# One output product by seven quarter products for tokens 512 to 1023, a rewritten first block, and two small edits in the gated products

## The chip, the cores and the metric

The kernel runs on one core of a Trainium2 chip. A core has TensorE (PE in the profile, with PEld for its weight loads) for matrix products, VectorE (DVE), ScalarE (ACT) and GpSimd (POOL) for element-wise work, and SyncE (SP), which issues the transfers here. The metric is the device time of one execution in microseconds. Three runs of the kernel before took 305.69, 305.70 and 306.51 us, median 305.7.

## The reference

Retention over 8 batches of 8 heads, 576 positions and 64 dimensions gives x, 4608 tokens of 512 values. A gated layer follows. In short:

```python
scores = q @ k.transpose(0, 1, 3, 2) / np.sqrt(64)
gamma = 1.0 - 2.0 ** (-5.0 - np.arange(8))
x = (scores * where(rel >= 0, gamma ** rel, 0)) @ v      # rel = i - j
gate = 1.0 / (1.0 + np.exp(-(x @ w_gate)))               # w_gate 512 x 1536
out = (gate * (x @ w_val)) @ w_out                       # w_val 512 x 1536, w_out 1536 x 512
```

All inputs and the output are float32 in memory; the products run on bfloat16 operands with float32 accumulation.

## The kernel before, in words

The sequence is cut into steps of 128 positions of one batch. Each step casts k, q and v (`casts_to`, lines 419 to 445), turns k and q with a DMA transposition on SP's queue or on TensorE (`turn_step`, L629), and takes part in an attention slot (`slot_of_two`, L739): "rows" are the scores within a step, "new" is what a step adds to the running state, "val" the values from the scores and from the state. These are matmuls of 64×64 tiles. After a slot, ScalarE casts the values off PSUM into x (`xT`, L780 and L786), and VectorE adds the states up (`add_state`, L827).

The gated layer goes over blocks of tokens. The first 512 tokens are done plainly: for each of 12 slices of 128 hidden columns, a gate product and a value product with 512 tokens each (`h_both`), a sigmoid on ScalarE into a tile `gv`, a multiplication on VectorE into the same tile, and then four output products of 12 matmuls with 512 columns (`op_first`). Tokens 512 to 767 and 768 to 1023 are two blocks of 256: `h_units` makes gates and values in pairs of slices, `op_units` makes two output products of 12 matmuls of 512 columns for each block and stores them. From token 1024 on the blocks have 512 tokens, and every product of four quarters is done as seven products of quarters on sums of operands, after Strassen and Winograd: `quarter_units` for gate ("g") and value ("w"), `quarters` (L1103) for the output. For these the operands have sums of their own: of x (`xsum`, L967), of the weights (`w_sums`, `wo_sums`, L364 and L323) and of gv (`gsum`, L941), each given to VectorE or to POOL.

In `quarters`, product 1 gathers in the bank qa. ScalarE copies it (L1177) into a second bank, qe, on which products 2, 5 and 3 go on adding, while 6, 7 and 4 go on in qa. VectorE adds the two banks to kept parts of products and leaves the output tile `ob`. The products come out in halves of six matmuls, and between halves other work can be put.

The order on each engine is the order in which the program writes the instructions. A run through the blocks takes one piece after the other out of `ffn_units`, and tables say what is put behind which piece: PAIRS_AT the attention slots of the first two small blocks, SUMS_AT the casts ("c"), turns ("t") and weight sums behind a piece, FIRST, ORDER and FINAL the sequence of gate and value quarters of a block of 512 ("g05" is the fifth product of the first unit of four slices; "0-1v" behind a colon is a sum of gv on VectorE), LATER and its like the sums of gv between output products. SP's queue holds loads, DMA transpositions and stores in one order.

In `quarter`, ScalarE's copy of the first product and a sigmoid that an earlier product left in `waiting` stand next to each other: `settle()` empties that list, and but for one place runs ahead of the copy.

## Time and profile before

| What | us |
|---|---|
| median of three runs | 305.7 |
| the profiled execution | 305.75 |
| its span, first to last instruction | 304.0 |
| granted TensorE clock, mean | 0.999 |
| TensorE busy | 296.8 |
| weight loads busy (beside it) | 250.0 |
| VectorE, ScalarE, POOL busy | 227.0, 204.9, 225.4 |

In the profile a group row reads: start, duration, engine, line, operation, output<-input, shape, count; what stands in brackets is how long the engine stood idle just before and what ended that. A group of pipelined matmuls lasts longer than the distance to the next group's start, since the last one's result comes some time after its last column; distances between starts say what a group keeps TensorE for. The first 21 us load and prepare; tokens 512 to 1023 are done between about 55 and 89 us, and the blocks of 512 tokens, some 30 us each, from 89 us to the end.

### The profile page before, as it was taken

The numbers are of one execution on the slowest core, as the hardware profiler recorded it, in microseconds if no ns is written. First come the engines' busy times: TensorE is split into PE (matmuls) and PEld (weight loads), VectorE is DVE, ScalarE is ACT, GpSimd is POOL, SyncE is SP. The second block draws the span as 40 slices with busy tenths as digits, with TensorE's granted clock in tenths as the row PEclk, the third lists the DMA queues.
The fourth block names the chain that finished last, engine by engine and source line by source line (L and its number), as shares of the span: only waits on it lengthen the run. The fifth ranks groups of instructions, "written<-read, shape, count | busy, mean of one in ns | idle before, by whom it ended". The sixth has DMA issues, their size and how long they took to land.

```text
span 304.0 us, 10670 instructions
## 1 busy us (share of the span) xinstructions
PE 296.8 (98%) x4429; PEld 250.0 (82%) x4437; DVE 227.0 (75%) x424; ACT 204.9 (67%) x414; POOL 225.4 (74%) x252
## 2 busy tenths in 40 slices
PE   8999999999999999999999999999999999999994
PEld 7677655978868888888888888888888888888884
DVE  5957776786886898588948983896489848945793
ACT  6755464335369657985798589857985698559830
POOL 5676544845679888999998999699969946960780
PEclk9999999999999999999999999999999999999999
DMA  7999999969999979998659966976694155004013
GB/s 212 303 360 394 316 351 220 209 149 204 200 198 203 262 133 222 223 205 237 99 125 213 261 144 141 228 188 141 122 201 132 38 119 195 4 2 138 2 37 104
DMA packets 145440, 54.99 MB, mean 181 GB/s; under 512 B 124400, under 2 KB 137712, under 8 KB 145392
## 3 DMA queue, kind: packets, MB, share of 16 engines
q1 hardware_dynamic: 144304, 53.59, 72.8%
q10 hardware_dynamic: 1088, 0.72, 0.8%
q8 instruction: 34, 0.56, 0.8%
q14 instruction: 14, 0.11, 0.1%
HBM read 37.75 MB, written 9.44 MB: 155 GB/s over the span
## 4 chain that ended last, share of the span: by engine, by line
PE 82%; POOL 7%; SPq 3%; DVE 3%; DMA 2%; issue 2%; ACT 1%; POOLq 0%
PE gatea L1013 10%; PE wa L1013 10%; PE qa L1136 9%; PE qe L1136 8%; PE gatee L1013 5%; PE we L1013 5%; PE h_v L884 4%; PE h_g L884 3%; PE op L1485 3%; PE hg L1335 3%; PE hv L1335 3%; SPq L186 3%; PE gateg L1013 3%; PE op L1267 3%; PE wg L1013 2%; DMA wg<-in_moe_w_gate_dram 2%
## 5 line engine op out<-in xcount | busy, mean ns | idle before, releaser
L1013 PEld LDWEIGHTS <-wg_sb 128*128 128x128 bf16 x336 | 32.9, 98 | 4.0
L1037 POOL TENSOR_TENSOR gv<-gv,wu 128x512 bf16<-128x512 bf16 x20 | 24.1, 1206 | 15.3 <-DVE wu L1050 15.3
L1136 PEld LDWEIGHTS <-gsum 128*128 128x128 bf16 x312 | 29.9, 98 | 3.7
L428 POOL TENSOR_TENSOR qk<-q,qtab 128x512 bf16<-128x512 f32 x28 | 30.2, 1079 | 2.7 <-DMA q<-in_q_dram 2.6
L1013 PEld LDWEIGHTS <-wv_sb 128*128 128x128 bf16 x296 | 28.9, 98 | 3.4
L1050 DVE TENSOR_TENSOR gu<-gatee,gu 128x512 f32<-128x512 f32 x21 | 14.5, 691 | 22.7 <-ACT gateg L1041 10.8
L1013 PEld LDWEIGHTS <-wgt_sb 128*128 128x128 bf16 x252 | 24.6, 98 | 3.7 <-issue 0.5
L941 POOL TENSOR_TENSOR gsum<-gsum,gv 128x256 bf16<-128x256 bf16 (+1 forms) x20 | 18.0, 911 | 12.8 <-DVE gsum L941 11.0
L1013 PE MATMUL gatea<-xsum,wg_sb 128*128 128x256 bf16 x168 | 25.0, 273 | 0.0
L1136 PEld LDWEIGHTS <-gv 128*128 128x128 bf16 x228 | 21.4, 98 | 3.5 <-DVE gv L1037 0.9
L428 POOL TENSOR_TENSOR qk<-k,ktab 128x512 bf16<-128x512 f32 x11 | 11.6, 1059 | 14.9 <-DMA k<-in_k_dram 12.6
L941 POOL TENSOR_TENSOR gsum<-gv,gsum 128x256 bf16<-128x256 bf16 (+1 forms) x24 | 21.9, 924 | 0.2
L702 DVE TENSOR_TENSOR pt<-row,tri 128x512 bf16<-128x512 f32 x30 | 19.2, 682 | 3.0 <-PE row L685 2.7
L1053 DVE TENSOR_TENSOR gs<-gatea,gs 128x512 f32<-128x512 f32 x21 | 14.5, 689 | 8.9 <-PE gatea L1013 8.8
L941 DVE TENSOR_TENSOR gsum<-gv 128x512 bf16<-128x512 bf16 (+1 forms) x34 | 19.9, 610 | 1.5 <-POOL gv L1037 1.5
L441 POOL TENSOR_TENSOR v<-v,ktab 128x512 bf16<-128x512 f32 x19 | 20.5, 1080 | 0.0
L657 ACT CAST sb<-s 128x512 bf16<-128x512 f32 (+1 forms) x26 | 14.4, 568 | 8.9 <-DVE s L827 8.7
L1013 PE MATMUL wa<-xsum,wv_sb 128*128 128x256 bf16 x136 | 20.4, 273 | 0.0
L786 ACT CAST xT<-val 128x512 bf16<-128x512 f32 x26 | 14.7, 592 | 6.8 <-PE val L732 6.8
L1013 PEld LDWEIGHTS <-wvt 128*128 128x128 bf16 x168 | 16.4, 98 | 2.1 <-issue 0.2
L1037 POOL TENSOR_TENSOR gv<-gv,ws 128x512 bf16<-128x512 bf16 x14 | 16.3, 1170 | 1.6 <-DVE ws L1053 1.4
L941 POOL TENSOR_TENSOR gsum<-gv 128x256 bf16<-128x256 bf16 (+1 forms) x20 | 17.5, 875 | 0.0
(202 smaller groups left out, 880.0 us busy)
## 6 DMA issues: line engine op xcount, KB each, us to landing
k<-in_k_dram SPq DMA_DIRECT2D x26, 256.0 KB, 3.9
q<-in_q_dram SPq DMA_DIRECT2D x26, 256.0 KB, 4.3
v<-in_v_dram SPq DMA_DIRECT2D x26, 256.0 KB, 4.9
out_dram<-ob SPq DMA_DIRECT2D x24, 256.0 KB, 2.9
wg<-in_moe_w_gate_dram SPq DMA_DIRECT2D x12, 256.0 KB, 5.5
wv<-in_moe_w_val_dram SPq DMA_DIRECT2D x12, 256.0 KB, 5.1
wo<-in_moe_w_out_dram SPq DMA_DIRECT2D x12, 256.0 KB, 5.3
v32p<-in_v_dram SPq DMA_DIRECT2D x6, 256.0 KB, 4.5
```

The lines of the kernel that those rows point to most:

```text
L428: eng.tensor_tensor(out=to, in0=by_halves(loaded[s][1 - i]), in1=tab, op=ALU.mult)
L441: nc.gpsimd.tensor_tensor(out=natural["v", s], in0=loaded[s][2], in1=tab, op=ALU.mult)
L702: nc.vector.tensor_tensor(out=t[:, y, 0:n].rearrange("p i m t -> p (i m) t"), in0=rows_tile[ss[0]][y][:, 0:n].rearrange("p i m t -> p (i m ...
L786: nc.scalar.copy(out=to, in_=src)
L884: nc.tensor.matmul(ps[:, i], lhsT=w_sb[:, kc, (fc + i) * P:(fc + i + 1) * P], rhs=xT(kc, slice(t0, t0 + n)), start=(kc == 0), stop=(kc == ...
L941: eng.tensor_tensor(out=to, in0=a, in1=b, op=op)
L1013: nc.tensor.matmul(ps[:, f], lhsT=w[:, kc, f * P:(f + 1) * P], rhs=x[:, kc], start=(first and f == 0 and kc == 0), stop=(f == 1 and kc == ...
L1037: eng.tensor_tensor(out=to, in0=to, in1=src, op=ALU.mult)
L1050: nc.vector.tensor_tensor(out=me["u2"], in0=e, in1=me["u2"], op=ALU.add)
L1053: nc.vector.tensor_tensor(out=me["s5"], in0=a, in1=me["s5"], op=ALU.add)
L1136: nc.tensor.matmul(ps[:, b], lhsT=left(fp)[:, b * P:(b + 1) * P], rhs=right(fp), start=(first and fp == 0 and b == 0), stop=(fp == NFC // ...
L1335: nc.tensor.matmul(ps[:, cols], lhsT=(wg_sb if what == "g" else wv_sb)[:, kc, fc * P:(fc + 1) * P], rhs=xT(kc, cols), start=(kc == 0), sto ...
```

## The change

Tokens 512 to 1023 still have their gates and values made in two blocks of 256, but into one common gv tile of 512 tokens. After the second block's gates and values one `quarters` call makes the output of all 512 tokens with seven products; `op_units` is gone. The sums of gv for it follow a new table, JOINT_AT. The slots of these tokens go by a table GROUPS: rows and new of steps 0 and 1, then the values of 0 and 1 by themselves, then rows and new of 2 and 3, and two slots of values and rows. The first block's program is one table of items, EARLY_AT, executed by `early`: D and d are a gate and a value product, C and o weight casts, "+" and "*" weight sums, p an output product, S, Z, I, J, X parts of the attention, s a store. Loads, casts and sums of steps 1 to 11 move (AHEAD, V_LATER, SUMS_AT), loads get fewer shared tiles from step 5 on, and sf's copies go to ScalarE.

Two edits concern the blocks from 1024 on: for products 1 and 5 of the first value unit (w0), ScalarE's copy now stands ahead of the waiting sigmoid (`behind_copy`), and the multiplication of product 4 of the third value unit (w24) is done in two halves.

```diff
-            t = landing([P, H, D], f"{nm}32_{s}", s >= 8)
+            t = landing([P, H, D], f"{nm}32_{s}", s >= 5)
...
-                (nc.vector.tensor_copy if hh == y else nc.sync.dma_start)(
+                (nc.scalar.copy if hh == y else nc.sync.dma_start)(
...
-    AHEAD = (2, 2, 1, 1, 0, 1, 1, 0, 1, 2, 1, 1)
+    AHEAD = (0, 3, 0, 0, 1, 1, 2, 0, 4, 3, 1, 0)
...
         for fc in fcs[::2]:
-            gv_tile(gvs, t0, fc)
-            both = made[t0, fc // 4][:, fc % 4:fc % 4 + 2, 0:n]
+            gv_tile(gvs, FIRST_PAIR, fc)
+            both = made[FIRST_PAIR, fc // 4][:, fc % 4:fc % 4 + 2, t0 - FIRST_PAIR:t0 - FIRST_PAIR + n]
...
-            if i != 1 or t0 != BLOCKS[2][0]:
+            behind_copy = i in (1, 5) and (t0 == BLOCKS[2][0] and i == 1 or (kind, u) == ("w", 0))
+            if not behind_copy:
                 settle()
...
-            def leaves(r, h, src, eng=nc.vector):
-                to = made[t0, u][:, 2 * r:2 * r + 2, h * 256:(h + 1) * 256]
-                if kind == "g":
-                    nc.scalar.activation(out=to, in_=src, func=AF.Sigmoid)
-                else:
-                    eng.tensor_tensor(out=to, in0=to, in1=src, op=ALU.mult)
+            def leaves(r, h, src, eng=nc.vector, parts=1):
+                for n in range(parts):
+                    part = slice(2 * n // parts, 2 * (n + 1) // parts)
+                    to = made[t0, u][:, 2 * r:2 * r + 2, h * 256:(h + 1) * 256][:, part]
+                    if kind == "g":
+                        nc.scalar.activation(out=to, in_=src[:, part], func=AF.Sigmoid)
+                    else:
+                        eng.tensor_tensor(out=to, in0=to, in1=src[:, part], op=ALU.mult)
...
-                leaves(1, 0, a)
+                leaves(1, 0, a, parts=2 if (kind, u) == ("w", 2) else 1)
+            if behind_copy:
+                settle()
...
-    FIRST = ("g01 g05 g11 w05 g06 g15 g03 w01 g02 g16 g12 g07 w06 g13 g21 g17 w03 w11 w07 g14 g04 w02 w04 "
...
+    FIRST = ("g01 g11 g05 w05 g06 g15 g03 w01 g16 g02 g12 g07 w06 g13 g17 g21 w03 w11 w07 g14 g04 w02 w04 w12 "
...
+    JOINT_AT = ("3:0-1v 4:0-2v 6:0-3v 8:0-4v 9:1-1v 12:2b1v 12:1-2v 13:2a1v 14:2a2p 14:2b2p 14:2-3p 15:1-4v "
+                "19:1-3p 20:2-4p").split()
...
-    def op_units(gvs, t0, n):
-        for nb in range(n // P):
...
-            gvs = {}
-            yield from h_units(gvs, range(NFC), t0, n)
-            yield from op_units(gvs, t0, n)
+            gvs = begun.setdefault(FIRST_PAIR, {})
+            sums = {}
+            for i, cols in enumerate(h_units(gvs, range(NFC), t0, n)):
+                behind(FIRST_PAIR, sums, JOINT.get((t0, i), ()))
+                yield cols
+            if t0 != FIRST_PAIR:
+                for i, cols in enumerate(quarters(gvs, sums, FIRST_PAIR, 2)):
+                    behind(FIRST_PAIR, sums, JOINT.get((t0, NFC + i), ()))
+                    yield cols
...
-    CUTS = 50
+    CUTS = 30
...
+    EARLY_AT = ("D2 D3 +g00v d3 Cv41v Cv43v d2 Cv40p D4 Cv42p D7 D5 +g01v +g03p D6 Cg81a Cg80p Cg82v Cg83v d4 "
...
+                "p5.0 p5.1 p5.2 p6.0 p6.1 p6.2 p7.0 p7.1 p7.2 p8.0 p8.2 p9.0 p8.1 p9.1 I p9.2 *20v J Z1 +g20p XO "
...
-    PAIRS_AT = ((0, 10), (0, 11), (1, 10), (1, 0))
...
+    GROUPS = [((0, 4), [], [0, 1]),
+              ((0, 6), [0, 1], []),
+              ((1, 1), [], [2, 3]),
+              ((1, 16), [2, 3], [4, 5]),
+              ((1, 20), [4, 5], [6, 7])]
```

Three places in the order of the instructions. The first is TensorE at the output product of tokens 512 to 767 before (op, behind the last value product h_v_10):

```order
L884 MATMUL h_v_10_1377<-xT_1089,wv_sb 128x256
L1267 LDWEIGHTS gv_0_1150
L1267 MATMUL op_0_1437<-wo_sb,gv_0_1150 128x512 [waits Activation_49]
L1267 LDWEIGHTS gv_0_1150
L1267 MATMUL op_0_1437<-wo_sb,gv_0_1150 128x256
```

and now, at the joint output product of tokens 512 to 1023 (qa and qe are the two banks, qk holds step 7's k and q):

```order
L1150 MATMUL qa_1726<-wo_sb,gv_2_1343 128x256
L1150 LDWEIGHTS gv_0_1140
L1150 MATMUL qe_1727<-wo_sb,gv_0_1140 128x256 [waits Activation_49]
L1150 LDWEIGHTS gv_0_1140
...
L1150 MATMUL qe_1727<-wo_sb,gv_1_1216 128x256
L630 LDWEIGHTS qk_1674 [waits Pool_49]
L630 MATMUL turn_0_1757<-ident,qk_1674 128x128
```

The plain products followed the values with the first gv tile as their one wait; now product 2 waits for ScalarE right behind product 1, and the turn of step 7 stands behind half of product 2.

The second place is ScalarE where x of tokens 768 to 1023 is cast off PSUM (the xT rows; h_g is a gate product, and glance reads a value tile's corner). Before:

```order
L916 COPY ob_1465<-op_0_1437 128x512 [waits PE_49,Activation_49]
L751 COPY glance<-val_1_1470 128x1 [waits PE_49]
L751 COPY glance<-val_0_1469 128x1
L780 COPY xT_1616<-val_0_1469 128x2x4x64 [waits PE_49,Activation_49]
L780 COPY xT_1616<-val_1_1470 128x2x4x64
L657 COPY sb_0_1630<-s_2_0_1618 128x512 [waits DVE_49,Activation_49]
```

and now:

```order
L892 ACTIVATE gv_2_1343<-h_g_8_1344 128x2x256 [waits PE_49]
L752 COPY glance<-val_1_1355 128x1 [waits PE_49]
L752 COPY glance<-val_0_1354 128x1
L781 COPY xT_1433<-val_0_1354 128x2x4x64 [waits PE_49,Activation_49]
L892 ACTIVATE gv_2_1343<-h_g_10_1435 128x2x256 [waits PE_49]
L781 COPY xT_1433<-val_1_1355 128x2x4x64
L892 ACTIVATE gv_0_1140<-h_g_0_1484 128x2x256 [waits PE_49]
```

The two casts stood together among output work; now the sigmoid of 512's last gate (h_g_10) stands between them, and the first gate of 768 (h_g_0) follows at once.

The third place is VectorE where the sums of x for the block from 1024 are made (xsum; pt is a masked row, s a state, ob an output tile). Before:

```order
L702 TENSOR_TENSOR pt_2111<-row_1_2044,tri 128x512
L323 TENSOR_TENSOR wt_sb<-wo_sb,wt_sb 128x512
L829 COPY s_3_0_2126<-new_0_2077 128x256 [waits PE_49]
L827 TENSOR_TENSOR s_3_0_2126<-s_3_0_2126,new_1_2078 128x256 [waits DVE_49]
L967 TENSOR_TENSOR xsum_0_2136<-xT_1949 128x512 [waits Activation_49]
```

and now:

```order
L703 TENSOR_TENSOR pt_2119<-row_1_2052,tri 128x512
L1167 TENSOR_TENSOR ob_2128<-qa_1726,s_512_1948 128x256 [waits PE_49,Activation_49]
L1167 TENSOR_TENSOR ob_2130<-qa_1726,s_512_1948 128x256
L830 COPY s_3_0_2142<-new_0_2085 128x256
L828 TENSOR_TENSOR s_3_0_2142<-s_3_0_2142,new_1_2086 128x256 [waits DVE_49]
L1167 TENSOR_TENSOR ob_1775<-qe_1727,s_512_1922 128x256 [waits PE_49]
L1167 TENSOR_TENSOR ob_1777<-qe_1727,s_512_1922 128x256
L972 TENSOR_TENSOR xsum_0_2153<-xT_1924 128x512 [waits Activation_49]
```

A sum of output weights has gone from this place, and four additions of the output of 512 to 1023 have come in ahead of the sums of x.

More of the change, by code (lines that the diff above doesn't have):

```diff
@@ L811, in after_two @@
                 add_state(s, 1)
-                if s < 2 * len(PAIRS_AT) and s == max(x for x in news if STEPS[x][1] < LAST):
+                if s < 8 and s == max(x for x in news if STEPS[x][1] < LAST):
                     ffn_psum.free_last(ffn_psum.held.pop())
@@ L1160, in places @@
             r = b // k
+            if t0 == FIRST_PAIR:
+                return [(slice(p0, p0 + w), slice(at, at + w)) for p0, at, w in rows(t0 + b * P, P)]
             return [(slice(p0 // 2, (p0 + w) // 2), slice(at + r, at + w, 2)) for p0, at, w in rows(t0 + b % k * 2 * P, 2 * P)]
@@ L1475 @@
-    cast_pair("q", 2, 1, nc.vector)
-    step(units, 2)
-    loads_to(1)
-    value_sums_begin()
-    for i in (0, 1, 3):
-        w_sums("w", i, 0, nc.vector)
-    def op_first(fcs, nbs, opps):
-        for fc in fcs:
-            for nb in nbs:
-                nc.tensor.matmul(opps[nb], lhsT=gvs[fc][:, nb * P:(nb + 1) * P], rhs=wo_sb[:, fc, :],
-                                 start=(fc == 0), stop=(fc == NFC - 1))
-    opps = [ffn_psum.tile([P, 512], FP32, tag="ffn", name=f"op_0_{nb}") for nb in range(3)]
@@ new lines, with out_product, first_running @@
+    ENGINES = {"p": nc.gpsimd, "v": nc.vector}
+    COPIES = {"p": on_pool, "v": on_dve, "a": on_act}
+    opps = []
+    def out_product(fc, nb):
+        if fc == 0:
+            pool, tag = (qk_psum, "qk") if nb == 3 else (ffn_psum, "ffn")
+            opps.append(pool.tile([P, 512], FP32, tag=tag, name=f"op_0_{nb}"))
+        nc.tensor.matmul(opps[nb], lhsT=gvs[fc][:, nb * P:(nb + 1) * P], rhs=wo_sb[:, fc, :],
+                         start=(fc == 0), stop=(fc == NFC - 1))
+    def first_running():
+        running[1] = new_state((1, 1, 1), FP32)
+        nc.vector.tensor_copy(out=running[1], in_=st_tiles[1])
+        keep_state((1, 1, 1), running[1], on_act)
```

210 lines of the change are left out of this document (82 added, 128 removed), and 7 rows, old and new, of tables (EARLY_AT, SUMS_AT).

## Prediction

> **What bounds the kernel now.** I read the page's busy times and chain first, then the table of stretches, then the order of time around the places that the change touches.
>
> ```profile
> PE 296.8 (98%) x4429; PEld 250.0 (82%) x4437; DVE 227.0 (75%) x424; ACT 204.9 (67%) x414; POOL 225.4 (74%) x252
> PE 82%; POOL 7%; SPq 3%; DVE 3%; DMA 2%; issue 2%; ACT 1%; POOLq 0%
> ```
>
> TensorE works 296.8 of 304.0 us and carries 82% of the chain that ended last; no other engine passes 75%. So time falls with columns through TensorE, or with its few waits. Where those are, the stretches show (columns: us, then busy time and count of PE, PEld, DVE, ACT, POOL, then clock, DMA share, GB/s):
>
> ```profile
> 20.00:40.00 20.00, 19.89 (x155) 14.68 (x156) 14.34 (x27) 11.67 (x22) 11.30 (x19) 1.00 1.03 363
> 40.00:60.00 20.00, 19.79 (x236) 13.59 (x237) 14.00 (x24) 9.84 (x19) 11.70 (x15) 1.00 1.00 250
> 60.00:70.00 10.00, 9.95 (x257) 8.00 (x257) 8.45 (x17) 4.33 (x10) 4.54 (x5) 1.00 0.80 176
> 80.00:90.00 10.00, 9.69 (x276) 6.34 (x277) 8.33 (x19) 5.34 (x11) 8.79 (x9) 1.00 0.95 208
> 90.00:100.00 10.00, 9.92 (x91) 8.91 (x91) 6.48 (x13) 9.67 (x20) 8.53 (x9) 1.00 0.95 196
> 120.00:200.00 80.00, 79.92 (x1176) 70.73 (x1174) 61.79 (x111) 64.22 (x130) 72.83 (x78) 1.00 0.87 185
> ```
>
> The clock is 1.00 throughout. TensorE has no idle time to win from 120 us on, and under 1 us between 20 and 100. Whatever the change wins must therefore be columns, or half-hidden losses inside busy time (a late operand shows as a long group, below). What it can lose are new waits, since little slack stands anywhere on this engine.
>
> **Part 1, the columns.** Tokens 512 to 1023 lose four plain products of 12 matmuls of 512 columns (24,576 columns) and get seven quarter products of 12 matmuls of 256 (21,504). What 12 such matmuls take is the distance between two groups with nothing between them:
>
> ```profile
> 112.71 1.47 PE L1136 MATMUL qa<-wt_sb,gsum 128*128 128x256 bf16 x12
> 114.02 1.47 PE L1136 MATMUL qe<-wt_sb,gsum 128*128 128x256 bf16 x12
> 139.05 1.54 PE L1136 MATMUL qa<-wo_sb,gv 128*128 128x256 bf16 x12
> 140.20 0.11 PEld L1136 LDWEIGHTS <-gv 128*128 128x128 bf16 x2 [0.18 <-DVE gv L1037]
> 140.52 0.32 PE L716 MATMUL val<-pt,v 64*64 64x64 bf16 x16
> 140.63 0.57 ACT L1177 COPY qe<-qa 128x512 f32<-128x512 f32 x1 [1.22 <-PE qa L1136]
> 141.78 1.49 PE L1136 MATMUL qe<-wo_sb,gv 128*128 128x256 bf16 x12
> ```
>
> 114.02 − 112.71 = 1.31 us, 109 ns for each. The 3,072 columns fewer are 12 such matmuls: **−1.31**.
>
> **Part 2, a new wait between products 1 and 2.** Product 2 adds onto a copy of product 1, which ScalarE makes (qe<-qa, 0.57 us). In the blocks before, an attention slot stands between the two (140.52 to 141.78), so the copy, which ends at 141.20, is hidden. In the new pair product 2 follows product 1 at once on TensorE, and the next other work, the turn of step 7, stands behind half of product 2. So TensorE waits: product 1's last column to the copy's start 0.11 to 0.19 (140.52 to 140.63, and the group's modelled end), 0.57 for the copy, 0.05 for the way back. **+0.81**; ends 0.7 and 0.9. If ScalarE still had a sigmoid before it, 0.6 more.
>
> **Part 3, a later x for tokens 768 to 1023.** Their x comes off PSUM by two ScalarE casts.
>
> ```profile
> 61.14 1.04 PE L884 MATMUL h_g<-xT,wg_sb 128*128 128x256 bf16 x8
> 62.10 0.45 PE L685 MATMUL row<-T 64*64 64x64 bf16 x32
> 62.21 0.60 ACT L887 ACTIVATE gv<-h_g 128x512 bf16<-128x512 f32 x1 [1.15 <-PE h_g L884]
> 67.70 2.79 PE L1267 MATMUL op<-wo_sb,gv 128*128 128x512 bf16 x23
> 67.96 1.07 ACT L780 CAST xT<-val 128x512 bf16<-128x512 f32 x2 [0.59 <-PE val L732]
> 70.33 1.04 PE L884 MATMUL h_g<-xT,wg_sb 128*128 128x256 bf16 x8
> ```
>
> Before, they run 67.96 to 69.03 beside plain output products, which keep TensorE until 70.33: 1.3 us of slack. Those products are gone. Afterwards the last work ahead of 768's first gate is h_v_10 (8 matmuls, 0.87), and on ScalarE the second cast stands behind the sigmoid of h_g_10. From the end of h_g_10: 0.19 to the sigmoid, 0.50 until the cast can start behind it (two casts take 1.07, one 0.57 to 0.59, so the pitch is 0.50), 0.59 for the cast, 0.05 back = 1.33, less the 0.87: **+0.46**; ends 0.3 and 0.6.
>
> **Part 4, the rewritten first block.** Weight casts and sums come sooner, sf copies go from VectorE to ScalarE, fewer matmuls are cut in two. The stretches 20 to 40 and 40 to 60 leave 0.11 and 0.21 idle, so it cannot win more than 0.3. Against it stand q casts on VectorE that now queue behind a multiplication or a store's copy, each good for one VectorE operation of 0.4 to 0.7 us at most where its cover fails. Nearest to the rows of little idle time I take **+0.15**, ends −0.3 and +0.4.
>
> **Part 5, more changes between tile sizes.** Two attention products that stood together now stand apart (S0/S1, I and Z1), and five slots serve where four did: three more trips from 128×128 to 64×64 matmuls and back. Above, h_g's eight matmuls should end at 61.14 + 8 × 0.109 = 62.01, and the 64×64 row starts at 62.10: 0.09 for the way in. Both ways on all three would be 0.54, none of it 0. I take the way in for two of them, **+0.2**, because the third follows a place where TensorE waits already.
>
> Here a rule speaks against the change. The Trainium skill, "TensorEngine Tiling (Array Packing)", section "Key Properties", says: "Mode switching requires drain". By it every one of the six changes would pay, 0.54 at the 0.09 of this trace, and the sum below would end at 305.9 rather than 305.6; the 0.09 at 62.01 agrees with it, and no row here shows the way out by itself.
>
> **Part 6, waits at the entry to the 512-token blocks.**
>
> ```profile
> 88.70 1.04 POOL L428 TENSOR_TENSOR qk<-k,ktab 128x512 bf16<-128x512 f32 x1 [0.18 <-DMA k<-in_k_dram]
> 88.76 1.60 DVE L967 TENSOR_TENSOR xsum<-xT 128x512 bf16<-128x512 bf16 x2
> 89.19 0.60 PE L1013 MATMUL gatea<-xT,wg_sb 128*128 128x256 bf16 x4
> 90.08 0.60 PE L1013 MATMUL gatee<-xsum,wgt_sb 128*128 128x256 bf16 x4 [0.28 <-DVE xsum L967]
> 90.28 0.41 DVE L967 TENSOR_TENSOR xsum<-xT,xsum 128x512 bf16<-128x512 bf16 x1
> 100.55 0.60 PE L1013 MATMUL gatea<-xsum,wgt_sb 128*128 128x256 bf16 x4
> 101.20 0.60 PE L1013 MATMUL we<-xsum,wvt 128*128 128x256 bf16 x4
> ```
>
> The gate sum of x comes 90.08 − 89.19 − 0.44 = 0.45 late, and the value product at 101.20 0.21 late by the same reckoning. The new order puts another product (g11, four more matmuls, 0.44) ahead of the later sums, and takes two weight sums off VectorE there; against that VectorE first adds four output halves of 0.4 us. Nearest to 0.66 less the part that stays behind those additions: **−0.55**, ends −0.66 and 0.
>
> **Part 7, one multiplication halved, one copy ahead of a sigmoid.** At 140.20 the weights of product 1's last two matmuls wait 0.18 for VectorE's last multiplication: 12 matmuls take 1.54, not 1.47, so 0.07 is lost, and alike in five blocks, the last at 261.92 (0.35). That operation becomes two:
>
> ```profile
> 261.92 0.11 PEld L1136 LDWEIGHTS <-gv 128*128 128x128 bf16 x2 [0.17 <-DVE gv L1037]
> 139.47 0.68 DVE L1037 TENSOR_TENSOR gv<-gv,wa 128x512 bf16<-128x512 bf16 x1
> 118.39 0.75 DVE L1153 TENSOR_TENSOR ob<-qa,s 128x256 f32<-128x256 f32 x2
> ```
>
> Two 256-wide additions take 0.75, so a first half would be done near 139.9 and the second at 140.22, 0.07 later than now; the eleventh matmul is freed, the twelfth keeps most of a wait of 0.03. So 0.04 in five blocks: **−0.2**, ends −0.35 and 0. The copy that goes ahead of the sigmoid is costed at 0: its reader on TensorE comes several products later, and the sigmoid's result has no reader on TensorE before the output products; if that cover fails, one ScalarE pitch of 0.5.
>
> **Part 8, who feeds step 7.** Its k and q are now wanted sooner.
>
> ```profile
> 75.60 0.53 SPq L171 DMA_DIRECT2D k<-in_k_dram  x1
> 80.12 1.16 POOL L428 TENSOR_TENSOR qk<-k,ktab 128x512 bf16<-128x512 f32 x1 [2.33 <-PE h_g L884]
> 81.23 1.04 POOL L428 TENSOR_TENSOR qk<-q,qtab 128x512 bf16<-128x512 f32 x1
> 83.99 0.61 PE L629 MATMUL turn<-ident,qk 128*128 128x128 bf16 x8
> k<-in_k_dram SPq DMA_DIRECT2D x26, 256.0 KB, 3.9
> L941 POOL TENSOR_TENSOR gsum<-gsum,gv 128x256 bf16<-128x256 bf16 (+1 forms) x20 | 18.0, 911 | 12.8 <-DVE gsum L941 11.0
> ```
>
> When 768's first gate starts, 24 plain matmuls (24 × 0.218 = 5.2) and one slot of rows (about 0.65, 62.10 to 62.75) fewer lie behind TensorE, and 0.46 more: 70.33 − 5.9 + 0.5 = 64.9. Twelve h groups (10.5), a slot (0.65), product 1 (1.31), the wait (0.81) and half of product 2 (0.65) put the turn at 78.8. SP takes its queue in order: k_7 stands behind transposition 5, and that behind step 6's six loads; I shift 75.60 forward by the 1.5 to 2.5 us that transpositions 2 to 4 come out sooner. 73.1 to 74.1, 3.9 to land, two casts of 1.04 one after the other: ready between 79.1 and 80.1, 0.3 to 1.3 behind the turn's place. I take the near end, **+0.3**, because POOL stood idle for 2.33 us ahead of these casts; ends 0 and 1.3.
>
> **The sum.** −1.31 + 0.81 + 0.46 + 0.15 + 0.2 − 0.55 − 0.2 + 0.3 = −0.14. Against the profiled execution's 305.75 us (span 304.0, with 1.75 around it) that is 305.6; the median of the runs shown is 305.7, so the two stand 0.05 apart. What a measurement of this kernel can tell from no change is about 0.3%, 0.9 us: below 304.8 is faster, above 306.6 slower. The columns saved are mostly paid back by two waits whose cover was the removed work itself.
>
> **The rivals.** *The columns count nearly in full*: parts 6 and 7 at their full 0.66 and 0.35, parts 4, 5 and 8 at 0, the two waits as they are: −1.31 + 1.27 − 1.01 = −1.05, 304.7; if ScalarE is early at 768's x too, 304.3. For it speaks that TensorE has 19.89 of 20 busy in the rewritten part, so switches may already be in the groups; against it the 0.09 at 62.01. *Step 7 comes late* (slower): if its q cast ends more than 1 us behind the turn's place at 78.8, TensorE stands 0.7 to 1.0 longer there than the 0.3 of part 8, and POOL's sums of gv for the later products (0.9 each) start behind the same casts and cost some 0.4: 305.6 + 1.2 = 306.8. For it speaks that POOL and SP work strictly in order and POOL is 8.79 of 10 busy in 80 to 90; against it the loads of steps 2 to 4, issued sooner. *The small edits do nothing*: halving frees no matmul, as the second half ends later than the whole did: 305.8.
>
> **How the numbers follow.** The forecast's own case 0.38 (304.9 to 306.3), columns in full 0.35, step 7 late 0.20, small edits without effect 0.07. The range 304.3 to 306.9 reaches to the low case's lower time and just over the high case's; what is left out are part 5 by the drain and part 8 late together, and early parts that win more than their idle time, under 2 in 10. Faster 0.35, the same 0.43, slower 0.22 (0.02 from the forecast's upper tail).
>
> **What would show it.** Right: one matmul fewer in the count; an idle stretch of about 0.8 ahead of the second product of the pair, released by ScalarE's copy; 0.4 to 0.5 ahead of 768's first gate, released by the cast of x; no wait of 0.28 for xsum; in the later blocks 1.50 rather than 1.54 for product 1. Wrong: TensorE idle over 1 us ahead of the turn of step 7 or of product 3, or blocks from 1024 on that last longer than before; or neither of the two new waits there, and a time below 304.3.

## The result

Six runs of the changed kernel took 308.6 to 311.0 us, median 309.6; six of the kernel before, beside them, 305.7 to 308.5, median 306.4. The ratio is 1.0123 (95% interval 1.0097 to 1.0150): slower by 1.2%, some 3.8 us by the ratio and 3.2 by the medians. The profiled execution took 309.63 us with a span of 307.9, against 305.75 and 304.0. Page of the changed kernel, busy times and chain:

```profile
PE 297.6 (97%) x4436; PEld 249.7 (81%) x4436; DVE 233.2 (76%) x446; ACT 207.5 (67%) x422; POOL 224.0 (73%) x249
PE 71%; ACT 1%; issue 0%; DVE 0%
```

TensorE has 3,072 columns fewer and is busy no less; the time came as idle time and as groups drawn out. The weight loads are one fewer (4,436 for 4,437), as forecast; of the matmuls of the kernel before eight records are missing. Where the time went, the same stretches show as before:

```profile
20.00:40.00 20.00, 20.00 (x136) 12.62 (x135) 14.19 (x28) 12.25 (x23) 11.44 (x18) 1.00 1.07 386
60.00:70.00 10.00, 9.71 (x201) 7.94 (x199) 9.31 (x17) 5.12 (x11) 6.88 (x7) 1.00 0.77 163
70.00:80.00 10.00, 9.14 (x79) 7.52 (x78) 9.90 (x17) 3.59 (x7) 5.74 (x6) 1.00 0.87 190
80.00:90.00 10.00, 8.06 (x272) 6.74 (x270) 7.93 (x19) 4.67 (x10) 8.84 (x10) 1.00 1.24 222
120.00:200.00 80.00, 80.00 (x1221) 71.04 (x1211) 61.41 (x115) 64.07 (x131) 70.45 (x76) 1.00 0.89 187
```

From 60 to 90 us TensorE is idle for 3.1 us (before: 0.05 in 60 to 70 and 0.31 in 80 to 90). VectorE, with 8.45 and 7.22 of 10 before, is now nearly full: 9.31 and 9.90 in 60 to 80. The kernel before had in the second of these stretches:

```profile
70.00:80.00 10.00, 10.00 (x93) 8.80 (x90) 7.22 (x14) 4.18 (x8) 5.42 (x6) 1.00 0.91 192
```

For the rest I go by starts of the same piece of work in both traces. TensorE's order of time in the changed kernel, the milestones and all its stands (times in which it does nothing) over 0.25 us behind the first of them:

```profile
38.15 0.38 PE L1456 MATMUL op<-wo_sb,gv 128*128 128x512 bf16 x1
52.65 1.04 PE L888 MATMUL h_g<-xT,wg_sb 128*128 128x256 bf16 x8
65.91 1.03 PE L888 MATMUL h_g<-xT,wg_sb 128*128 128x256 bf16 x8 [0.29 <-ACT xT L781]
71.49 1.03 PE L888 MATMUL h_v<-xT,wv_sb 128*128 128x256 bf16 x8 [0.32 <-DVE gv L894]
78.69 1.47 PE L1150 MATMUL qa<-wo_sb,gv 128*128 128x256 bf16 x12 [0.32 <-DVE gv L894]
80.86 0.81 PE L1150 MATMUL qe<-wo_sb,gv 128*128 128x256 bf16 x6 [0.70 <-ACT qe L1193]
85.47 0.22 PE L733 MATMUL val<-T,sb 64*64 64x64 bf16 x3 [0.83 <-issue]
89.41 0.25 PE L733 MATMUL val<-T,sb 64*64 64x64 bf16 x6 [0.41 <-ACT sb L658]
93.54 1.04 PE L1018 MATMUL gatea<-xT,wg_sb 128*128 128x256 bf16 x8
112.47 1.47 PE L1150 MATMUL qa<-wo_sb,gv 128*128 128x256 bf16 x12
```

The same milestones in the kernel before (the one at 89.19 stands in the prediction):

```profile
38.29 0.38 PE L1485 MATMUL op<-wo_sb,gv 128*128 128x512 bf16 x1
51.96 1.04 PE L884 MATMUL h_g<-xT,wg_sb 128*128 128x256 bf16 x8
108.61 1.47 PE L1136 MATMUL qa<-wo_sb,gv 128*128 128x256 bf16 x12
```

| Stretch, from start to start | before | changed | difference |
|---|---|---|---|
| to the first output product | 38.29 | 38.15 | −0.14 |
| to 512's first gate | 13.67 | 14.50 | +0.83 |
| to 1024's first gate ("the pair's stretch") | 37.23 | 40.89 | +3.66 |
| to 1024's first output product | 19.42 | 18.93 | −0.49 |
| to the end of the span | 195.39 | 195.43 | +0.04 |

So the pair's stretch, which has 1.31 us fewer columns, takes 3.66 more: 4.97 us are to be found there. A stand costs its idle time and about 0.16 more, since the profile counts the pipelined tail of the last matmul as busy: 0.70 idle at 80.86, but product 1 had its last column at 78.69 + 1.31 = 80.00, so 0.86. With that the six stands named above and one of 0.21 at 72.74 (a gate waits for VectorE's state) come to 4.2; the other 0.8 is in groups drawn out, around slots and elsewhere (from the value product at 73.61 to the next group it is 1.05, where 0.87 is usual).

### The profile page after: what moved, and what is told of

The parts are those of the page before. It is cut to its first block, busy times and chain, and to the rows that moved or that the text cites. A ratio compares the mean times of both kernels' runs of the same rounds, so it can differ in the third digit from the quotient of the medians.

```text
span 307.9 us, 10715 instructions
## 1 busy us (share of the span) xinstructions
PE 297.6 (97%) x4436; PEld 249.7 (81%) x4436; DVE 233.2 (76%) x446; ACT 207.5 (67%) x422; POOL 224.0 (73%) x249
## 4 chain that ended last, share of the span: by engine, by line
PE 71%; ACT 1%; issue 0%; DVE 0%
PE gatea L1018 12%; PE qa L1150 12%; PE wa L1018 11%; PE qe L1150 10%; PE gatee L1018 6%; PE we L1018 6%; PE gateg L1018 3%; PE wg L1018 3%; PE qa L1228 2%; PE val L733 2%; PE val L717 2%; PE row L686 1%; PE h L1078 1%; PE new L694 1%; PE qf L1150 0%
## 5 line engine op out<-in xcount | busy, mean ns | idle before, releaser
L1150 PEld LDWEIGHTS <-gsum 128*128 128x128 bf16 x360 | 34.5, 98 | 4.3
L946 POOL TENSOR_TENSOR gsum<-gsum,gv 128x256 bf16<-128x256 bf16 (+1 forms) x22 | 18.8, 869 | 16.2 <-DVE gsum L946 14.0
L1150 PEld LDWEIGHTS <-gv 128*128 128x128 bf16 x264 | 25.3, 98 | 4.4 <-issue 1.4
L946 POOL TENSOR_TENSOR gsum<-gv,gsum 128x512 bf16<-128x512 bf16 (+1 forms) x25 | 23.0, 929 | 0.2
L946 DVE TENSOR_TENSOR gsum<-gv 128x512 bf16<-128x512 bf16 (+1 forms) x40 | 21.7, 566 | 1.1 <-POOL gv L1045 1.1
L946 POOL TENSOR_TENSOR gsum<-gv 128x256 bf16<-128x256 bf16 (+1 forms) x21 | 18.7, 892 | 0.0
```

Of the source, the lines that this page charges most:

```text
L946: eng.tensor_tensor(out=to, in0=a, in1=b, op=op)
L1150: nc.tensor.matmul(ps[:, b], lhsT=left(fp)[:, b * P:(b + 1) * P], rhs=right(fp), start=(first and fp == 0 and b == 0), stop=(fp == NFC // ...
```

## The experiments

All are compared with the kernel before, run on the same chip beside them; for places, I use the pair's stretch, 40.89 in the changed kernel and 37.23 in the kernel before.

**The two small edits alone, on the kernel before.**

```diff
-            if i != 1 or t0 != BLOCKS[2][0]:
+            behind_copy = i in (1, 5) and (t0 == BLOCKS[2][0] and i == 1 or (kind, u) == ("w", 0))
+            if not behind_copy:
                 settle()
...
-                leaves(1, 0, a)
+                leaves(1, 0, a, parts=2 if (kind, u) == ("w", 2) else 1)
+            if behind_copy:
+                settle()
```

> The kernel before, with only the two small edits of the blocks from 1024 on (ScalarE's copy ahead of the waiting sigmoid in w0, the last multiplication of w24 in two halves). Theory: the halving frees TensorE in product 1, so that the 12 matmuls of product 1 take 1.47 us again instead of 1.54 in each of six blocks: 0.2 to 0.45 us less than the kernel before, about 305.4 to 305.6 where the kernel before has 305.8. Rival: the second half ends later than the whole did and TensorE gains nothing: within 0.1 of the kernel before, product 1 still at 1.50 to 1.54.

305.25 us against 305.82, ratio 0.9981 (0.9959 to 1.0002). TensorE's first output product of the second block of 512:

```profile
140.55 1.47 PE L1140 MATMUL qa<-wo_sb,gv 128*128 128x256 bf16 x12
```

It is 1.47 rather than 1.54, and so in the four blocks behind it, so the halving does free TensorE. What the copy ahead of the sigmoid does by itself was not tried. The time fell by 0.6 by the medians, with an interval that just touches none; the theory's 0.2 to 0.45 lies in it. What these edits are not is the cause of the loss.

**The slot between products 1 and 2.**

```diff
-              ((1, 16), [2, 3], [4, 5]),
+              ((1, 13), [2, 3], [4, 5]),
...
-1.14:t07v
+1.16:t07v
```

> The changed kernel, with the slot of values 2, 3 and rows 4, 5 moved from behind half of product 6 to between products 1 and 2 of the pair, and the turn of step 7 from between the halves of product 2 to behind half of product 6. Theory: TensorE's stand ahead of product 2 (0.70 idle, 0.86 from start to start) is there only because nothing lies between, so it goes to 0, and the idle 0.83 behind the slot goes or stays by itself: 0.8 to 1.7 us less than the changed kernel, 308.0 to 308.8. Rival: the slot's VectorE work comes ahead of the sums of gv, product 6 waits for them instead, and no more than 0.3 is won.

308.28, ratio 1.0088 (1.0055 to 1.0121). The stand ahead of product 2 and the one in the slot are gone. But from 53.42 to 94.22 it is 40.80, as long as before, for others have come:

```profile
76.34 1.03 PE L888 MATMUL h_g<-xT,wg_sb 128*128 128x256 bf16 x8 [0.89 <-DVE gv L894]
80.98 1.47 PE L1150 MATMUL qa<-wo_sb,gv 128*128 128x256 bf16 x12 [0.87 <-DVE gv L894]
83.80 0.31 PE L733 MATMUL val<-T,sb 64*64 64x64 bf16 x12 [0.26 <-DVE glance L754]
86.81 0.38 PE L630 MATMUL turn<-ident,qk 128*128 128x128 bf16 x4 [0.40 <-ACT xT L787]
```

The theory was right on the cause of the stand at product 2. The two largest of the new stands are no price of the move: they come ahead of the moved slot, and the execution that was traced took 309.80, with a median of 308.28. The median is 1.3 lower than the changed kernel's, as the theory has it, with intervals that overlap.

**Five weight sums later, to relieve VectorE.**

```diff
-0.7:g23v  0.9:o03v  1.0:o23v  1.8:w02v  1.13:g12v
+2.20:g23v 1.19:o03v 1.20:o23v 2.8:w02v  2.6:g12v
```

> The changed kernel, with five weight sums taken out of VectorE's crowded stretch and made later (two sums of output weights for product 4 from the first pieces of 768 to product 7, three sums of gate and value weights to the block from 1024). Theory: VectorE is full between 66 and 80 us (9.90 of 10 busy in 70 to 80), and TensorE's three stands there (0.32, 0.21 and 0.32 idle, each some 0.16 more from start to start, 1.3 in all) are its doing: two of three go, 0.8 to 1.3 us less than the changed kernel, 308.3 to 308.9. Rival: VectorE's delay comes from the chain of masks and states behind the rows, not from the weight sums, and the stands stay within 0.2; or the sums only move the stand to the block from 1024.

309.59, ratio 1.0125 (1.0099 to 1.0151): nothing won. Two of the three stands at VectorE are gone, but the same two are gone from the traces of the next two trials, which leave VectorE's work there as it was; so that the sums made them is not shown. The stretch is 41.33: one stand of 0.23 has come earlier, the stand in the slot is longer (0.92), and a new one stands at 90.44:

```profile
89.26 0.25 PE L733 MATMUL val<-T,sb 64*64 64x64 bf16 x6 [0.41 <-ACT sb L658]
90.44 0.32 PE L733 MATMUL val<-T,sb 64*64 64x64 bf16 x16 [0.52 <-DVE glance L754]
```

**The first block's order mended.**

```diff
-S0 p4.0 p3.1 p4.1 S1 Z0
+p4.0 p3.1 p4.1 S0 S1 Z0
...
-p9.1 I p9.2 *20v J Z1
+p9.1 p9.2 I *20v J Z1
...
-s0v p0.3 c0
+c0 s0v p0.3
```

> The changed kernel, with the first block's order mended at three places: the two score products S0 and S1 together, the products I and Z1 together, and the casts of step 0 ahead of VectorE's copy of the first output tile. Theory: the stretch from the first output product to the first gate of 512 takes 14.50 us against 13.67 in the kernel before because of two more trips between tile sizes (some 0.2 each) and a turn that waits 0.20 idle, 0.36 from start to start, for a q cast: 0.6 to 0.8 less, the stretch at 13.7 to 13.9, 308.8 to 309.0. Rival: a trip costs next to nothing and only the turn's 0.36 goes: 14.1.

307.86, ratio 1.0077 (1.0052 to 1.0102). The stretch from the first output product to 512's first gate:

```profile
37.86 0.38 PE L1456 MATMUL op<-wo_sb,gv 128*128 128x512 bf16 x1
51.53 1.04 PE L888 MATMUL h_g<-xT,wg_sb 128*128 128x256 bf16 x8
92.01 1.04 PE L1018 MATMUL gatea<-xT,wg_sb 128*128 128x256 bf16 x8
```

51.53 − 37.86 = 13.67, the kernel before to the hundredth: the whole 0.83 is these three places. The turn's stand was 0.36 of it, so the two trips to 64×64 tiles cost some 0.23 each. The median fell by 1.8, more than the theory allows; the other 0.9 is not explained.

**What the profile gives to nothing.** The 0.83 at 85.47 stands in the middle of a slot, at a matmul that waits for no semaphore.

```diff
-    for n, pieces in zip(FILLS, (4, 2, 1)):
+    for n, pieces in zip(FILLS, (1, 2, 1)):
```

> The changed kernel, with the 40 idle matmuls of 128 columns at the start made 10 of 512 columns: the same columns, 60 rows fewer in TensorE's instruction stream, nothing else touched. It asks what the idle 0.83 us is that the profile gives to nothing (issue), in the middle of the slot behind half of product 6, at one and the same instruction in three traces (0.83, 0.92, 1.06). Theory: TensorE's instructions come in blocks of 256 rows, and there the next block is late, since the slot uses up rows fastest of all and transfers stand still around it; with the block's edge 60 rows later it falls in the next slot's start and the stand is gone, 0.8 to 1.1 us less, 308.5 to 308.8, the idle of 0.41 ahead of the next slot's state perhaps back at another size. Rival: something that the slot itself waits for, a transposition or a semaphore that the profile does not name: the stand is still at that instruction, at 0.8 to 1.1, and the time the same as the changed kernel.

309.59, ratio 1.0129 (1.0095 to 1.0164). The edit puts 10 idle matmuls at the start for 40, with the same columns, so TensorE's instructions (two rows to a matmul) are 60 fewer ahead of the slot. With that the stand is gone, and the time is not. TensorE's stands after 80 us:

```profile
80.48 0.82 PE L1150 MATMUL qe<-wo_sb,gv 128*128 128x256 bf16 x6 [0.70 <-ACT qe L1193]
81.84 0.62 PE L630 MATMUL turn<-ident,qk 128*128 128x128 bf16 x8 [0.54 <-POOL qk L428]
88.92 0.25 PE L733 MATMUL val<-T,sb 64*64 64x64 bf16 x6 [0.35 <-ACT sb L658]
92.34 1.47 PE L1150 MATMUL qa<-wt_sb,gv 128*128 128x256 bf16 x12 [0.46 <-DVE s L828]
```

TensorE now waits for POOL's casts of step 7 and for a VectorE state. The first of these waits comes ahead of the slot: two stands of 0.32 at VectorE's multiplications are gone in this trace, so TensorE reaches the turn sooner. VectorE's rows fit that. The same sum of gv, in the changed kernel and here:

```profile
72.61 1.07 DVE L946 TENSOR_TENSOR gsum<-gsum,gv 128x512 bf16<-128x512 bf16 x1
72.94 0.42 DVE L946 TENSOR_TENSOR gsum<-gsum,gv 128x512 bf16<-128x512 bf16 x1
```

In the changed kernel POOL casts step 6's k from 72.35 to 73.39, here only from 74.56 on, when that k has come by DMA. A sum of weights a little earlier likewise takes 1.23 there and 0.41 here. So which stands a trace has seems to depend on where VectorE's sums meet POOL's work. Where the 0.83 came from is taken up in the last section.

**Both casts of x ahead of the sigmoid.** The first trial put the values' slot at (0, 5).

```diff
-              ((0, 6), [0, 1], []),
+              ((0, 5), [0, 1], []),
```

> The changed kernel, with the slot of values 0 and 1 one piece earlier, so that both casts of x for tokens 768 to 1023 stand ahead of the sigmoid of 512's last gate on ScalarE. Theory (part 3 of the prediction): the stand ahead of 768's first gate, 0.29 idle and 0.46 from start to start, is the second cast's place behind that sigmoid, and goes to 0. Rival: the values then wait for the masks on VectorE, and the same 0.3 to 0.5 turns up ahead of the slot.

Three pieces of the slot at (0, 4) come first, so the order was left as it was, and this was a second look at the changed kernel: 308.93, stretch 40.84, the stands at the same seven places (0.29, 0.32, 0.21, 0.19, 0.70, 1.18, 0.41). The second trial moved that slot:

```diff
-    GROUPS = [((0, 4), [], [0, 1]),
+    GROUPS = [((0, 3), [], [0, 1]),
```

> The changed kernel, with the rows of steps 0 and 1 one piece earlier, so that the values follow one piece earlier and both casts of x for 768 to 1023 stand ahead of the sigmoid of 512's last gate (the earlier trial of this left the order as it was, since the slot's three following pieces were not yet through). Theory (part 3): the stand ahead of 768's first gate, 0.29 idle and 0.45 from start to start, goes to 0. Rival: the rows or values wait in their new place for a transposition, a mask or a state, 0.3 to 0.5.

311.21 in one run, stretch 41.25. The stand ahead of 768's first gate is gone, so its cause is shown; the rival's price is there too, at a row that waits for VectorE's copy of turned k and q (T):

```profile
59.59 0.32 PE L686 MATMUL row<-T 64*64 64x64 bf16 x16 [0.86 <-DVE T L632]
```

**Several together.** The edits on slot, sums, first block and idle matmuls:

> The changed kernel with four of the edits together: the slot between products 1 and 2, the five weight sums later, the first block's order mended, and 10 idle matmuls for 40. Theory: the gains add where they are at different places: 0.83 in the first block, 0.86 at product 2, 1.0 in the slot, 0.4 ahead of the next, less 0.7 of new waits at the turn and the slot; with 309.6 for the changed kernel that makes 306.8 to 307.3, still above the kernel before. Rival: what is left is VectorE's and POOL's supply between 66 and 90 us, which takes back what the covers give: 308 and more.

309.81, ratio 1.0143 (1.0103 to 1.0182), stretch 40.19. The rival holds. One stand of 1.69 idle takes back what the covers gave, and VectorE's order of time shows why:

```profile
81.17 0.31 PE L733 MATMUL val<-T,sb 64*64 64x64 bf16 x12 [1.69 <-DVE glance L754]
78.67 1.26 DVE L946 TENSOR_TENSOR gsum<-gsum,gv 128x512 bf16<-128x512 bf16 x1
79.86 1.12 DVE L946 TENSOR_TENSOR gsum<-gv 128x256 bf16<-128x256 bf16 x1
80.91 0.21 DVE L754 TENSOR_SCALAR glance<-val,val 128x1 f32<-128x1 f32 x1
```

The look at the value tile, on which the slot's last matmuls wait, stands behind the joint product's sums of gv. With the looks on ScalarE, and the rows one piece earlier:

```diff
-    LOOK_ACT = (0, 3, 5,
+    LOOK_ACT = (0, 2, 3, 4, 5,
...
-1.14:t07v
+1.17:t07v
```

> The changed kernel with everything that the traces so far name taken out together: slot between products 1 and 2 with the turn of step 7 behind product 6, five weight sums later, the first block's order mended, 10 idle matmuls for 40, the first two slots' rows one piece earlier (so that both casts of 768's x come ahead of a sigmoid), and the two looks at the value tiles of steps 2 and 4 on ScalarE rather than at the end of VectorE's queue. Theory: what costs is a set of separate waits of TensorE between 52 and 94 us; without them that stretch comes down from 40.9 to 37.0 to 38.0, and the time to 305.0 to 306.5, level with the kernel before. Rival: VectorE and POOL supply too late for the joint product wherever the waits are put, and the stretch stays over 39, the time over 307.5.

308.19, ratio 1.0088 (1.0063 to 1.0114), stretch 40.35: again the rival. The longest wait is that of the rows moved forward (first line); behind it TensorE now waits for the sums themselves, three times (0.35, 0.23, 0.30), while POOL is full (last line, the stretch 84 to 90), and 0.49 for a ScalarE copy:

```profile
56.03 0.32 PE L686 MATMUL row<-T 64*64 64x64 bf16 x16 [0.80 <-DVE T L632]
81.82 0.39 PE L1150 MATMUL qa<-wt_sb,gsum 128*128 128x256 bf16 x2 [0.35 <-POOL gsum L946]
89.07 0.61 PE L1150 MATMUL qe<-wo_sb,gsum 128*128 128x256 bf16 x4 [0.30 <-POOL gsum L946]
84.00:90.00 6.00, 4.97 (x143) 3.84 (x141) 5.97 (x11) 3.16 (x8) 6.00 (x7) 1.00 0.98 223
```

The same with the weight sums left where they were:

> The same kernel as the one with everything taken out, but with the five weight sums left in VectorE's crowded stretch. Theory: with the other waits gone VectorE's load shows: one to three stands of TensorE at gv between 66 and 80, 0.5 to 1.5 us more than without the sums. Rival: the sums cost nothing, as in the trial where they alone were moved: within 0.3.

308.25, ratio 1.0102 (1.0063 to 1.0141), stretch 39.08. Where those five sums stand makes no difference that these runs can tell.

**The block from 1024 in the kernel before.** First one swap, then the changed kernel's whole order of it, both with the two small edits.

```diff
-    FIRST = ("g01 g05 g11 w05
+    FIRST = ("g01 g11 g05 w05
```

> The kernel before, with the two small edits and one swap in the block from 1024: product g11 ahead of g05, as the changed kernel has it. Theory: the stand of 0.28 idle, 0.45 from start to start, at the sum of x is covered by the four matmuls moved ahead, and the changed kernel's stretch from 1024's first gate to its first output product (18.93 against 19.42) comes from this: 0.4 to 0.5 less than with the small edits alone, 304.7 to 305.0, and under both kernels. Rival: VectorE's sum of x is late by more than one product, or the wait comes back at a later one: 305.2 to 305.5.

> The kernel before with the two small edits and the changed kernel's whole order of gate, value and gv sums for the block from 1024 (tables FIRST and LATER_FIRST). Theory: the changed kernel's 0.49 us in the stretch from 1024's first gate to its first output product comes from this order, which covers both the sum of x and the later wait at a value product: 18.95 to 19.1 rather than 19.38 to 19.42, 0.3 to 0.45 less than with the small edits alone, 304.8 to 305.2 against 305.8. Rival: it comes from the weight sums that were made sooner, and in the kernel before the same order waits for them: 19.3 to 19.6, no gain.

306.00, ratio 1.0002 (0.9986 to 1.0018), and 305.54, ratio 0.9989 (0.9969 to 1.0009). From 1024's first gate to its first output product it takes 19.38 and 19.39; the second:

```profile
88.61 1.04 PE L1013 MATMUL gatea<-xT,wg_sb 128*128 128x256 bf16 x8
108.00 1.47 PE L1140 MATMUL qa<-wo_sb,gv 128*128 128x256 bf16 x12
```

So the 0.45 at xsum goes, but in both traces three later products start 0.1 late each, a value product 0.3 rather than 0.2, and the changed kernel's 18.93 isn't in the order. What is left is the work that was made sooner, weight sums above all; that is argued, not shown. With three of these sums put back the stretch took 19.16 in two traces and 18.94 in a third. What unloaded this stretch loaded the one ahead of it.

**Without the sums of gv.** The joint product reads gv itself; the kernel leaves out the 14 sums that the output of tokens 512 to 1023 needs, and the columns are the same.

```diff
         def summed(i):
-            return lambda fp: sums[fp // 2][i // 2][:, i % 2, fp % 2]
+            return raw(i // 2, i % 2) if t0 == FIRST_PAIR else lambda fp: sums[fp // 2][i // 2][:, i % 2, fp % 2]
...
-                behind(FIRST_PAIR, sums, JOINT.get((t0, i), ()))
...
-                    behind(FIRST_PAIR, sums, JOINT.get((t0, NFC + i), ()))
```

Left out of the changed kernel:

> The changed kernel without the 14 sums of gv for the joint product: its seven products read gv itself, so the output of tokens 512 to 1023 is left wrong; the columns and every other instruction stay. Theory: the joint product costs what it does because its own operand sums come on VectorE and POOL just where these also cast k, q, v and make masks and states (POOL busy 6.00 of 6 us from 84 to 90, VectorE 5.43 of 6 from 78 to 84): without them the stretch from 512's first gate to 1024's first gate falls from 40.9 to 38.0 to 39.3 (the copy at product 2 and the cast of x still cost 0.86 and 0.45, the late block of instructions 0.8), and the time to 307.0 to 308.3. Rival: the sums are hidden, the stands are the fixed ones alone, and the stretch stays over 40.

308.39, ratio 1.0083 (1.0051 to 1.0114), stretch 40.70. By the stretch the rival holds, and the median is just above the theory's 308.3: in the changed kernel itself the sums are hidden behind the stands, the 1.32 below among them.

```profile
84.23 0.22 PE L733 MATMUL val<-T,sb 64*64 64x64 bf16 x3 [1.32 <-issue]
```

Left out of the kernel with every edit together (looks on ScalarE, five sums later):

> The kernel with everything taken out, again without the 14 sums of gv (output of tokens 512 to 1023 wrong). Theory: with covers in place and no sums to wait for, TensorE's stretch comes down from 39.1 to 40.4 to 36.5 to 37.5, that is to the columns and the slots, and the time to 304.5 to 305.8: under or level with the kernel before. Rival: what saturates VectorE and POOL there is the work of the attention steps alone, and the stretch stays over 38.5.

```profile
51.50 1.04 PE L888 MATMUL h_g<-xT,wg_sb 128*128 128x256 bf16 x8
89.32 1.04 PE L1018 MATMUL gatea<-xT,wg_sb 128*128 128x256 bf16 x8
```

89.32 − 51.50 = 37.82, against 40.35 and 39.08 with the sums: here they cost 1.3 to 2.5, one trace each, and the stands at POOL's sums are gone with them. The theory's 36.5 to 37.5 is missed by stands of 0.80 and 0.34 at rows that wait for turned q and k. The time does not follow (307.36 to 312.15 in four runs, ratio 1.0173, 1.0117 to 1.0229; the profiled execution was the 307.36). From 1024's first gate to the end its trace takes 216.0 us, that of the changed kernel 214.4 and that of the kernel before 214.8; the other three runs, which are 2.3 to 4.8 longer and have no trace, had a granted clock of 0.988 to 0.993. Why was not settled, so of the kernels with several edits at once I use the stretch alone. The last kernel also reads plain output weights and makes nine sums later:

> As the last, and the joint product also reads plain output weights, so that nine of the twelve sums of output weights go back to the block from 1024, where the kernel before has them (output of tokens 512 to 1023 wrong). Theory: the sums of weights cost TensorE up to 0.5 us beside the sums of gv: the stretch is 36.0 to 37.0, 1024's own stretch 19.0 to 19.4 again. Rival: they are hidden wherever they stand, and the stretch is within 0.2 of the kernel without sums of gv alone.

311.18, ratio 1.0179 (1.0136 to 1.0223). The stretch is 37.53, 0.3 less than with these sums in it; 1024's own stretch then takes 22.87, with waits of TensorE of up to 1.52 there. So their 0.3 stands beside the 1.3 to 2.5 of the sums of gv, and is no more than executions differ by.

## Why the prediction was wrong

Forecast were 305.6 us, range 304.3 to 306.9, slower at 0.22. It became 309.6. Step by step:

- **Part 1, the columns, −1.31: not to be seen whole.** Without the stands the changed kernel's stretch would be 40.89 − 4.2 = 36.7, 0.5 under the kernel before. The missing 0.8 is in groups drawn out; how much of it slots take (part 5) was not worked out.
- **Part 2, +0.81: right.** 0.70 idle, 0.86 from start to start, by ScalarE's copy; moving the slot there took it away. The way back, 0.05, for which the prediction shows no row, is in the trace now: the copy ends at 80.81, product 2 starts at 80.86.
- **Part 3, +0.46: right.** 0.29 idle, 0.45 from start to start, and the way back is 0.05 again (65.86 to 65.91); with both casts ahead of the sigmoid it went.
- **Parts 4 and 5, +0.35: wrong in size.** The first block lost 0.83, all of which three edits gave back; of that the q cast was 0.36 and two trips 0.23 each. I had taken 0.09 for a trip, the way in alone. The way out can be read in the kernel before too, contrary to what I wrote: 32 row matmuls take 0.28 (62.10 to 62.38), 32 of "new" start at 62.38 and the next value product at 62.75, so 0.09 is left; a trip is 0.18 by these rows. The Trainium skill, "TensorEngine Tiling (Array Packing)", "Key Properties", says that changing the tiling mode drains TensorE; the trace agrees, at both ends of a trip.
- **Part 6, −0.55: right size (−0.49), wrong cause.** The product moved ahead does nothing by itself (19.38 and 19.39 against 19.42). The gain is left with the work made sooner, by exclusion, and that was paid for one stretch earlier.
- **Part 7, −0.2: right way, a little small.** The twelfth matmul keeps no wait: 1.47, not 1.50, for 1.54, which is 0.07 in five blocks, 0.35. From 1024's first output product to the end three traces of the kernel before with these edits take 195.1 to 195.2, where it has 195.39; two traces of the changed kernel have 195.43 and 195.14, so there the gain is not sure.
- **Part 8, +0.3 at the turn: right on the supply, hidden in the changed kernel.** TensorE was itself so late (81.51 rather than 78.8) that the casts were ready; with two stands fewer ahead of it the turn waited 0.54 for POOL.
- **What the sum left out.** Stands at VectorE's multiplications and states (0.32, 0.21, 0.32 idle), at ScalarE's state casts (0.41), which queue behind copies of products, and the one that the profile gives to nothing (0.83): 2.9 us with their tails. For none of them I had a term. Every sign of being right that I had named came (the stands at product 2 and at 768's first gate, no wait at xsum, a shorter product 1), and none of those of being wrong: both lists held only terms that I had. I costed the sums of gv and the sums of weights only where they left, in part 6, and named no cover where they arrived; part 8 gave POOL the one late operand. VectorE's busy time in 60 to 80 went from 15.67 to 19.21 us, and TensorE waited for it at one place or another in every trace with the sums. There the sums are also dear. VectorE in the changed kernel, and one row of POOL:

```profile
76.33 0.41 DVE L946 TENSOR_TENSOR gsum<-gv,gsum 128x512 bf16<-128x512 bf16 x1
76.67 1.37 DVE L364 TENSOR_TENSOR wv_sb<-wv_sb 128x512 bf16<-128x512 bf16 x1
76.36 1.39 POOL L323 TENSOR_TENSOR wt_sb<-wo_sb,wt_sb 128x512 bf16<-128x512 bf16 x1
77.96 0.67 DVE L894 TENSOR_TENSOR gv<-gv,h_v 128x512 bf16<-128x512 bf16 x1
```

A sum of two bfloat16 tiles takes 0.41 where it starts ahead of POOL's own sum, and the next one 1.37, to 78.04, with POOL's sum running from 76.36 to 77.75; the multiplication behind it, 0.67, came 0.32 idle too late for TensorE. The Trainium skill, "SBUF — State Buffer", "Who interferes with whom", says that an instruction of VectorE with two inputs in this memory contends with POOL's reads; these rows agree.

The rival "step 7 comes late" named the right engines and the wrong place. What the runs show is two layers: separate waits in front, and behind them VectorE and POOL, which do not make the joint product's 14 sums beside casts, masks and states in time. Removing the first layer alone leaves the stretch at 39.1 to 40.4, removing the sums alone leaves 40.7, and only both together brought 37.8 and 37.5. That holds for this stretch; no version brought the time itself back.

| The pair's stretch, one trace each | us |
|---|---|
| kernel before; with the small edits; with the swap; with the order | 37.23; 39.21; 37.36; 37.02 |
| changed kernel, twice | 40.89; 40.84 |
| slot moved; sums later; first block mended; idle matmuls fewer; x first | 40.80; 41.33; 40.48; 40.75; 41.25 |
| several; every edit; every edit but the five sums | 40.19; 40.35; 39.08 |
| no sums of gv: alone; with every edit; and plain output weights | 40.70; 37.82; 37.53 |

One of the kernel before's kind took 39.21, by two stands at VectorE (1.08 and 0.47 idle) that the others do not have; that execution took 307.02, the longest of its twelve, where the median was 305.25, while those of 39.08 and 37.82 were the shortest of their kernels. So differences under 2 us between single traces of this stretch say little. The causes of the stands at product 2, at 768's first gate and in the first block rest on stands that went with their edit; that of the rest on the two traces without sums. No version was surely faster than the kernel before; the two small edits on it come nearest (0.9981).

## What to carry to other kernels

A product by seven quarters trades matmul columns for operand sums on the element-wise engines: before counting the columns, add up what those engines already do in the very stretch where the sums would have to be made, at the price they have beside each other. When a wait is taken out and the time stays, look who is waited for next: here it was mostly the same two full engines. And for every sum "made sooner", cost the place where it arrives as well as the one it leaves.

## What was not expected of the hardware

TensorE stood for 0.77 to 1.32 us at the same matmul of a 64×64 slot in six traces of kernels that share that order (0.83, 0.92, 1.06, 1.18, 0.77, 1.32), with no semaphore to wait for. It did not where 60 rows had been taken out of its stream far ahead. The page shows 34 transfers of instructions, 0.56 MB, in one queue; if that queue is TensorE's, the 8,872 rows that the page lists for it make about 260 to a transfer. The slot uses some 240 rows in 1.4 us. That would fit a block of instructions that comes late; which transfer it waited for the trace doesn't show.

In all six traces the data transfers stood nearly still just then (some 10 GB/s from 83.6 to 84.8 in the changed kernel's, and TensorE went on 0.5 us after they had resumed). In the trial with 60 rows fewer they did not stand still there at all (87 GB/s and more from 80 to 87), so the trial doesn't tell a late block from whatever held the transfers. That they stood still is not enough by itself: with the slot moved between products 1 and 2 they did so from 83.6 to 84.8 too (4 to 27 GB/s), and TensorE had no stand without a named cause. So the instruction stream is the likelier cause, or both together; neither is shown alone.

The Trainium skill, "Runtime: NRT & Kernel Launch", "Instruction fetch mechanics", gives blocks of 256 instructions and calls the cost of crossing one "mostly hidden". The count of some 260 rows to a transfer agrees about; if the stand is such a crossing, it was not hidden in this slot.
